# Transposes of gathered rows placed by routing groups instead of at fixed steps, in a fused recurrence and mixture-of-experts kernel

## The chip, the cores and the metric

The kernel runs on one core of one Trainium2 chip. The metric is the device time in microseconds of one execution, as the median of several runs. A core has five engines with queues of their own: TensorE (PE, with its weight loads as PEld), VectorE (DVE), ScalarE (ACT), GpSimd (POOL) and SyncE (SP); transfers are issued from these queues to 16 DMA engines.

## What is computed

A gated recurrence over four sequences of 5056 tokens gives a row of 256 numbers for each of 20224 tokens. A router then assigns every token to one of eight experts, each taking exactly 2528 tokens, the highest logits first. Each expert is a two-layer network with 1024 hidden units.

```python
sig = 1.0 / (1.0 + np.exp(-f_logit))
f = lower_bound + (1.0 - lower_bound) * sig
for t in range(S):
    h = f[:, t] * h + (1 - f[:, t]) * x[:, t]
    y[:, t] = h
...
logits = x @ w_gate                     # x: the rows y, N = 20224
for idx in np.argsort(-logits.flatten()):
    tok, e = idx // E, idx % E
    if assigned[tok] >= 0 or counts[e] >= N // E:
        continue
    assigned[tok] = e
    counts[e] += 1
...
for e in range(E):
    mask = assigned == e
    out[mask] = np.maximum(x[mask] @ w1[e], 0.0) @ w2[e]
```

## The kernel before

**Stages.** The recurrence runs until about 165 us and leaves its rows in `hbuf` in device memory. The expert stage follows and fills the rest. Products are computed with operands split in a high and a low part (`xh`, `xl`; `w1h`, `w1l`; `hh`, `hl`; the two halves of `w2s`), so each layer takes several matmuls.

**Chunks and steps.** The tokens of an expert `k` are worked in chunks `(k, c)` of up to 512 (four tiles of 128): six chunks for experts 0 and 7, five for the others, 42 in all. A chunk has eight steps `j`, one for each block of 128 hidden units. The main loop (line 1455) counts the 336 steps as `i`. Step `i` issues `first(k, c, j)`, six matmuls into a bank `pw` of three, whose result ScalarE and VectorE move out as `hh` and `hl`; then the second layer of a step that lies up to three back (`LAG`, line 1428), `second(...)`, which adds into four banks `py`, one for each tile. So a chunk's last addition falls in step 2 of the chunk after it; there ScalarE and VectorE empty the `py` banks (`y`), and in step 3 the next chunk's second layer writes them again. `second` also puts the stores of the finished rows in the list `issues`.

**Rows for a chunk.** `gather` (line 1118) puts one transfer per tile in `issues`. It is called up to two chunks ahead. `issue` (line 1035) pops entries from that list, mostly one at the end of a step, tied to the latest evacuation of `pw`. The rows land in `xg`, of which there are three. `trans(k, c, h)` (line 1164) turns half `h` of a chunk's rows: four transposes on TensorE into one more `pw` bank, written out by ScalarE as `xh` and by VectorE as `xl`. For `h == 0` it first issues what gathers of the chunk are still in the list. A chunk of two tiles is turned whole in one call, and the call for `h == 1` returns. The loop calls `trans` for the next chunk in fixed steps: 3 and 5 (`TJ`), or 5 and 6 (`T0`) in the first and last chunk of experts 0 and 1 (lines 1478 to 1481). Between a chunk's first turn and its next chunk's start lie a few steps.

**Routing beside the experts.** The assignment for the later experts is computed while the earlier ones run. Generators (`route`, `compact`, the weight split `split`) are wrapped in `Bg`; each `yield` names the engine that its next piece starts with and the tiles that it needs. `tick` (line 1435), called at several places inside `first` and `second` and at the end of a step, lets a generator go on when a model of the engines' time, `Pace`, says that the inputs are there. Pieces that name PE issue the routing groups: 20 or 23 short matmuls `rt<-O,MK` of a threshold search, the single ones `rt<-CR,tot` and `rt<-Z,onesr`, the counts `rt<-cnt,...`, and one to three placement matmuls `rt<-RA,g`. A new `Bg` starts with the need `("PE",)`, though its first piece may issue no matmul.

**Evacuations.** `post` and `flush` hold the evacuations back until `Pace` finds their input ready, or until two steps later. The order on every engine is the order in which the program issues: there is no other reordering.

All instructions are recorded from one helper, so every row of the profile carries line 109; they are told apart by their tiles.

Of the kernel before, what the change touches and what calls it, by code (L numbers as in the profile page):

```python
# [115 lines left out]
def kernel(ctx: ExitStack, tc: tile.TileContext, x: bass.AP, f_logit: bass.AP,  # L116
# [878 lines left out]
    with tc.manual_schedule(engines={mybir.EngineType.PE, mybir.EngineType.DVE, mybir.EngineType.Activation}):  # L995
        moe(ctx, tc, locals())


def moe(ctx, tc, g):
# [30 lines left out]
    issues = []  # L1030

    gate = []
    SYNC = mybir.DependencyInfo(mybir.DependencyClass.Sync, mybir.DependencyReason.DATA)

    def issue(n=1, upto=None, paced=False):
        st = None
        if upto is not None:
            n = max([x + 1 for x, (what, _) in enumerate(issues) if upto(what)], default=0)
        for _ in range(min(n, len(issues))):
            st = issues.pop(0)[1]()  # L1040
            if paced and gate:

                tc.add_manual_dep(st.ins, gate[-1].ins.name, SYNC, reason="one transfer per step")
        return st
# [25 lines left out]
    def split(k):  # L1070
        if k:
            issue(upto=lambda what: what == ("w", k))
# [37 lines left out]
    def tiles(k, c):  # L1110
        b, n = CHUNKS[k][c]
        return [min(P, CAP - (b + q) * P) for q in range(n)]
# [26 lines left out]
    posts, step = [], 0  # L1139

    def post(eng, tiles, emit, up=None, now=False):

        p = Post(eng, tiles, emit, up)
        posts.append(p)
        if now:
            flush(step)
        return p.done if now else p

    def flush(upto=-9):
        for p in list(posts):  # L1150
            if p.at <= upto or p.ready():
                p.done = p.emit() or True
                posts.remove(p)

    def turn2(t):
        return t.rearrange("p m (a b) -> p m a b", a=2)

    def pairs(t):
        return t.rearrange("p m (b a) -> p m a b", a=2)
# [4 lines left out]
    def trans(k, c, h, now=False):  # L1164
        ns = tiles(k, c)
        w, m = sum(ns), 2 if len(ns) <= 2 else 1
        if h == 0:
            issue(upto=lambda what: what == ("g", k, c))
            XS[k, c] = (xp.tile([P, 2, 512], F32R, name="xh"), xp.tile([P, 2, 512], F32R, name="xl"))
        elif m == 2:  # L1170
            return
        xh, xl = (turn2(t)[:, h:h + m, :, :w // 2] for t in XS[k, c])
        if now:
            def part(q):
                pt = pws.tile([P, 512], F32R, name="pw")
                pt = pt[:, :2 * P].rearrange("p (m w) -> p m w", m=2)
                for i in range(2):
                    nc.tensor.transpose(pt[:, i], XG[k, c][:, q, i * P:(i + 1) * P], ident_r)
                pt = pairs(pt.bitcast(F32))
                qh, ql = (t[:, :, :, q * P // 2:(q + 1) * P // 2] for t in (xh, xl))  # L1180
                up = post("ACT", (pt,), lambda: nc.scalar.activation(qh, pt, AF.Copy), None, now)
                post("DVE", (xh,), lambda: v.tensor_tensor(ql, pt, qh.bitcast(F32), op=OP.subtract), up, now)
            return [part(q) for q in range(2)]
        pt = pws.tile([P, 512], F32R, name="pw").rearrange("p (m w) -> p m w", m=m)
        for q, n in enumerate(ns):
            for i in range(m):
                nc.tensor.transpose(pt[:, i, q * P:q * P + n], XG[k, c][:n, q, (h + i) * P:(h + i + 1) * P],
                                    ident_r[:n, :n])
        pt = pairs(pt.bitcast(F32)[:, :, :w])
        up = post("ACT", (pt,), lambda: nc.scalar.activation(xh, pt, AF.Copy), None, now)  # L1190
        return post("DVE", (xh,), lambda: v.tensor_tensor(xl, pt, xh.bitcast(F32), op=OP.subtract), up, now)

    def first(k, c, j):
        w = sum(tiles(k, c))
        w1h, w1l, _ = WS[k]
        xh, xl = XS[k, c]
        ps = pws.tile([P, 512], F32, name="pw")
        mm = [(w1h, xh, 0), (w1h, xl, 0), (w1l, xh, 0), (w1h, xh, 1), (w1h, xl, 1), (w1l, xh, 1)]
        if (k, c) == (0, 0):
            mm = [(w, x, h) for w, x in ((w1h, xh), (w1l, xh), (w1h, xl)) for h in range(2)]  # L1200
        for i, (a, b, h) in enumerate(mm):
            nc.tensor.matmul(ps[:, :w], a[:, h, j], woven(turn2(b)[:, h, :, :w // 2]), start=(i == 0), stop=(i == 5))
            if i in (1, 3):
                tick()
        hh = hp.tile([P, 512], F32R, name="hh")
        hl = hp.tile([P, 512], F32R, name="hl")
        def evacuate():
            gate.append(nc.scalar.activation(hh[:, :w], ps[:, :w], AF.Relu))
        up = post("ACT", (ps,), evacuate)
        post("DVE", (hh,), lambda: v.scalar_tensor_tensor(hl[:, :w], ps[:, :w], 0.0, hh[:, :w].bitcast(F32),  # L1210
                                                          op0=OP.max, op1=OP.subtract), up)
        HS[k, c, j] = hh, hl
# [45 lines left out]
    def second(k, c, j):  # L1258
# [19 lines left out]
        for q, n in enumerate(ns):  # L1278
# [3 lines left out]
            if q:  # L1282
                tick()
# [20 lines left out]
            if q % 2 == 0:  # L1304
                turn = len(SC) // 2 + sum(what[0] == "s" for what, _ in issues) // 2
                issue(upto=lambda what: what[0] == "s" and what[1] <= turn - BEHIND)
                Y[q // 2] = yp.tile([P, 2, D], F32, name="y")
# [14 lines left out]
    class Bg:  # L1322
# [3 lines left out]
        def tick(self, force=False, within=None):  # L1326
            if self.done:
                return False
            if within is not None:
                self.wait = min(self.wait, int(within))  # L1330
            wants = bank in self.need
            if not force:
                if self.wait:
                    self.wait -= 1
                    return False
                if wants and bank.holder not in (None, self):
                    return False
                tiles = [t for t in self.need[1:] if t is not bank]
                if not pace.due(self.need[0], [*tiles, *bank.last] if wants else tiles, TIGHT if closing else SLACK):
                    return False  # L1340
            if wants:
                while bank.holder not in (None, self):
                    bank.holder.tick(True)
                bank.holder = self
            try:
                self.need = next(self.gen)
                self.wait = self.apart
            except StopIteration:
                self.done = True
            return True  # L1350

        def until(self, ok):
            while not ok():
                self.tick(True)

    comp, prog = {}, {}

# [19 lines left out]
    def have(k, what, n=1):  # L1377
        return k in prog and prog[k].get(what, 0) >= n
# [45 lines left out]
    order = [(k, c) for k in range(E) for c in range(len(CHUNKS[k]))]  # L1424
# [5 lines left out]
    TJ, T0 = (3, 5), (5, 6)  # L1430
# [24 lines left out]
    for i in range(len(todo) + LAG):  # L1455
        step = i
        flush(i - 2 if i < len(todo) else i)
        if i < len(todo):
            k, c, j = todo[i]
            if (c, j) == (0, 0) and k:  # L1460
                assert wn == k + 1
                sp.until(lambda: sp.done)
                sp = None
            first(k, c, j)
            if not sp0.done:
                flush()
            sp0.tick(True)
            tick()
            NS = len(CHUNKS[k])
            if gathers:  # L1470

                kk, cc = gathers[0]
                ahead = order.index((kk, cc)) - order.index((k, c))
                if ahead == 1 and j >= 1 or ahead == 2 and j >= (2 if (k, c) == (0, 0) else 0) and have(
                        kk, "ids", sum(CHUNKS[kk][cc])):
                    gather(kk, cc, (1, 4) if (kk, cc) == (0, 2) else None, soon=ahead == 1 or c == len(CHUNKS[k]) - 2 and j > 0)
                    gathers.pop(0)
            at = T0 if k < 2 and c in (0, NS - 1) else TJ
            nxt = order.index((k, c)) + 1
            if j in at and nxt < len(order):  # L1480
                trans(*order[nxt], at.index(j))
        while made < first_lag.get(i, i - LAG + 1):
            second(*todo[made])
            made += 1
        issue(1 if i < len(todo) else 99, paced=i < len(todo))
        tick()
# [30 lines left out]
```

## Time and profile before

| | us |
|---|---|
| median of 3 runs | 1104.24 |
| lowest and highest | 1103.49, 1104.25 |
| the profiled execution | 1103.94 |
| its span, first to last instruction | 1102.2 |
| TensorE busy in the span | 1083.9 (98%) |
| VectorE busy | 802.7 (73%) |
| ScalarE busy | 534.3 (48%) |
| GpSimd busy | 445.5 (40%) |

The profile is of one execution. Busy time is the union of an engine's instructions; a matmul's row is longer than the time for which it holds the queue, because matmuls overlap. So for TensorE the difference between one start and the next is read, not the length of a row. In a timeline, like instructions in a row are merged in one row with their count, and the row's start is that of the first.

### The profile page before, as it was taken

The numbers are of one execution on the slowest core, as the hardware profiler recorded it, in microseconds if no ns is written. First come the engines' busy times: TensorE is split into PE (matmuls) and PEld (weight loads), VectorE is DVE, ScalarE is ACT, GpSimd is POOL, SyncE is SP. The second block draws the span as 40 slices with busy tenths as digits, with TensorE's granted clock in tenths as the row PEclk, the third lists the DMA queues.
The fourth block names the chain that finished last, engine by engine and source line by source line (L and its number), as shares of the span: only waits on it lengthen the run. The fifth ranks groups of instructions, "written<-read, shape, count | busy, mean of one in ns | idle before, by whom it ended". The sixth has DMA issues, their size and how long they took to land.

```text
span 1102.2 us, 21571 instructions
## 1 busy us (share of the span) xinstructions
PE 1083.9 (98%) x8193; PEld 958.5 (87%) x8193; DVE 802.7 (73%) x2048; ACT 534.3 (48%) x1223; POOL 445.5 (40%) x428
## 2 busy tenths in 40 slices
PE   8999998999999999999999999999999999999998
PEld 6888787999988898888888888888888888898897
DVE  7999878878877896789678877887787664334333
ACT  7999775332732454245424642364226573323322
POOL 6777405332533333344333333433343433333332
PEclk9999998999999999999999999999999999999999
DMA  9999794112111311131113111311112211111110
GB/s 373 410 398 385 270 383 159 54 38 99 60 48 44 114 49 48 39 119 58 44 43 114 48 48 44 117 51 48 43 61 106 98 71 52 47 48 52 44 52 38
DMA packets 36524, 121.74 MB, mean 110 GB/s; under 512 B 7746, under 2 KB 7748, under 8 KB 35524
## 3 DMA queue, kind: packets, MB, share of 16 engines
q0 software_dynamic: 18992, 58.22, 15.3%
q1 hardware_dynamic: 17424, 62.14, 14.4%
q8 instruction: 64, 1.05, 0.4%
q14 instruction: 40, 0.33, 0.1%
q10 hardware_dynamic: 4, 0.00, 0.0%
HBM read 78.92 MB, written 41.42 MB: 109 GB/s over the span
## 4 chain that ended last, share of the span: by engine, by line
PE 91%; DMA 3%; issue 2%; DVE 1%; ACT 1%; POOL 1%; POOLq 0%; ACTq 0%; DVEq 0%
PE py L109 39%; PE pw L109 39%; PE rt L109 4%; PE pb L109 2%; PE pf L109 2%; PE pl L109 2%; PE pr L109 2%; DMA fl<-in_f_logit_dram 1%; DMA xg<-hbuf,gid 1%; DMA r<-in_moe_w_dram,wi 1%; DVE gk L109 0%; DVE fl L109 0%; ACT fl L109 0%; POOL xg L109 0%; DVE MK L109 0%
## 5 line engine op out<-in xcount | busy, mean ns | idle before, releaser
L109 PE MATMUL py<-w2s,hh 128*128 128x512 f32 (+3 forms) x1448 | 453.3, 365 | 0.0
L109 ACT ACTIVATE hh<-pw 128x512 fp32r<-128x512 f32 (+3 forms) x336 | 192.3, 572 | 439.9 <-PE pw L109 400.3
L109 PE MATMUL py<-w2s,hl 128*128 128x256 f32 (+1 forms) x1280 | 349.3, 273 | 0.0
L109 DVE SCALAR_TENSOR_TENSOR hl<-pw,hh 128x512 fp32r<-128x512 f32 (+3 forms) x336 | 219.0, 654 | 127.3 <-ACT hh L109 126.2
L109 PEld LDWEIGHTS py<-w2s,hh 128*128 128x128 f32 (+1 forms) x1448 | 261.3, 188 | 26.3
L109 POOL DMA_INDIRECT out_dram<-y,ids x160 | 161.1, 1007 | 271.9 <-ACT hh L109 143.2
L109 POOL DMA_INDIRECT xg<-hbuf,gid x160 | 161.5, 1009 | 270.9 <-ACT hh L109 211.1
L109 PE MATMUL pw<-xh,w1l 128*128 128x512 f32 (+3 forms) x672 | 249.3, 373 | 0.0
L109 PE MATMUL pw<-xl,w1h 128*128 128x512 f32 (+3 forms) x672 | 249.0, 373 | 0.0
L109 PE MATMUL pw<-xh,w1h 128*128 128x512 f32 (+3 forms) x672 | 248.3, 372 | 0.5 <-ACT xh L109 0.5
L109 PEld LDWEIGHTS py<-w2s,hl 128*128 128x128 f32 (+1 forms) x1280 | 243.1, 190 | 4.3
L109 PEld LDWEIGHTS pw<-xh,w1h 128*128 128x128 f32 x672 | 127.8, 191 | 16.0 <-ACT xh L109 0.7
L109 PEld LDWEIGHTS pw<-xh,w1l 128*128 128x128 f32 x672 | 127.8, 191 | 13.3
L109 PEld LDWEIGHTS pw<-xl,w1h 128*128 128x128 f32 x672 | 128.5, 192 | 6.9
L109 POOL TENSOR_TENSOR xl<-fl,xl 128x1024 f32<-128x1024 f32 (+2 forms) x39 | 91.2, 2347 | 27.5 <-DVE A L109 5.3
L109 DVE TENSOR_TENSOR_SCAN gk<-fg,gk,pb 128x512 f32<-128x512 f32 (+3 forms) x68 | 81.6, 1239 | 9.3 <-PE pb L109 6.9
L109 ACT ACTIVATE y<-py 128x256 f32<-128x256 f32 (+2 forms) x151 | 52.7, 409 | 71.6 <-PE py L109 65.4
L109 DVE TENSOR_TENSOR y<-py,y 128x256 f32<-128x256 f32 (+1 forms) x139 | 52.7, 418 | 41.3 <-ACT y L109 41.0
L109 ACT ACTIVATE junk<-rt,r 128x158 bf16<-128x158 f32 x155 | 59.2, 396 | 15.4 <-DVE R L109 11.4
L109 ACT ACTIVATE fg<-pf,nomlb 128x512 f32<-128x512 f32 (+1 forms) x80 | 53.9, 690 | 9.1 <-DVE gk L109 4.0
L109 DVE TENSOR_TENSOR xl<-pw,xh 128x512 fp32r<-128x512 f32 (+3 forms) x81 | 54.1, 667 | 0.2 <-ACT xh L109 0.2
L109 ACT ACTIVATE xh<-pw 128x512 fp32r<-128x512 f32 (+3 forms) x81 | 47.6, 587 | 3.8 <-PE pw L109 3.8
(224 smaller groups left out, 1255.4 us busy)
## 6 DMA issues: line engine op xcount, KB each, us to landing
fl<-in_f_logit_dram SPq DMA_DIRECT2D x39, 512.0 KB, 7.4
xl<-in_x_dram SPq DMA_DIRECT2D x39, 512.0 KB, 6.6
hbuf<-hr SPq DMA_DIRECT2D x39, 512.0 KB, 4.5
xg<-hbuf,gid POOLq DMA_INDIRECT x160, 2.7
out_dram<-y,ids POOLq DMA_INDIRECT x160, 2.4
r<-in_moe_w_dram,wi POOLq DMA_INDIRECT x25, 5.0
fl<-in_f_logit_dram SPq DMA_DIRECT2D x1, 256.0 KB, 8.0
xl<-in_x_dram SPq DMA_DIRECT2D x1, 256.0 KB, 6.2
```

The lines of the kernel that those rows point to most:

```text
L109: r = self.pace.last[self.name] = f(*args, **kw)
```

## The change

The steps 3 and 5 become windows. When step 0 of a chunk has run, two entries are put in a list `turns`, one for each half of the next chunk, with a first and a last step: 2 to 4 and 4 to 6, or exactly 5 and exactly 6 where `early` holds. Each time a `Bg` has issued a piece whose need named PE, `join` looks at the head of the list: if its first step has come and the chunk has `landed`, which means that its last gather was issued at least two steps ago and none is left in `issues`, the half is turned at once, directly behind that piece. The other half cannot follow before the next step. A half that finds no such piece is turned in its last step, behind `first` as before, and a `tick` follows it. `issue` notes for every chunk the step of its latest gather.

```diff
+    issued = {}
+
     def issue(n=1, upto=None, paced=False):
...
-            st = issues.pop(0)[1]()
+            what, emit = issues.pop(0)
+            st = emit()
+            if what[0] == "g":
+                issued[what[1:]] = step
...
+            small = self.need[0] == "PE"
             try:
                 self.need = next(self.gen)
                 self.wait = self.apart
             except StopIteration:
                 self.done = True
+            if small:
+                join()
             return True
...
+    turns = []
+
+    def landed(kc):
+        return issued.get(kc, step) <= step - 2 and not any(what == ("g", *kc) for what, _ in issues)
+
+    def join():
+        if turns and turns[0][0] <= step and landed(tuple(turns[0][2:4])):
+            turn_next()
+
+    def turn_next():
+        trans(*turns[0][2:])
+        turns.pop(0)
+        if turns:
+            turns[0][0] = max(turns[0][0], step + 1)
...
-            at = T0 if k < 2 and c in (0, NS - 1) else TJ
             nxt = order.index((k, c)) + 1
-            if j in at and nxt < len(order):
-                trans(*order[nxt], at.index(j))
+            if j == 0 and nxt < len(order):
+                early = k < 2 and c in (0, NS - 1)
+                for h, (a, b) in enumerate(((5, 5), (6, 6)) if early else ((2, 4), (4, 6))):
+                    turns.append([i + a, i + b, *order[nxt], h])
+            if turns and turns[0][1] <= i:
+                turn_next()
+                tick()
```

## Rows read from the trace of the kernel before

**Rows 1.** The page: TensorE's busy time, its granted clock in slices, the chain by engine.

```profile
PE 1083.9 (98%) x8193; PEld 958.5 (87%) x8193; DVE 802.7 (73%) x2048; ACT 534.3 (48%) x1223; POOL 445.5 (40%) x428
...
PEclk9999998999999999999999999999999999999999
...
PE 91%; DMA 3%; issue 2%; DVE 1%; ACT 1%; POOL 1%; POOLq 0%; ACTq 0%; DVEq 0%
```

**Rows 2.** Waits of TensorE's weight loads, 196 to 1098 us: total us, times, longest.

```profile
PEld rt L109 <- DVE CR L109: 0.4, 1, 0.4
```

**Rows 3.** Timeline of TensorE (start, length in us, instruction): a routing group alone.

```profile
565.18 0.38 PE L109 MATMUL pw<-xl,w1h 128*128 128x512 f32 x1
565.40 0.76 PE L109 MATMUL rt<-O,MK 128*128 128x64 bf16 x20
566.00 0.46 PE L109 MATMUL pw<-xh,w1l 128*128 128x512 f32 x1
566.30 0.38 PE L109 MATMUL pw<-xh,w1h 128*128 128x512 f32 x1
```

**Rows 4.** Timeline of TensorE: four transposes alone, between the two layers.

```profile
563.29 0.46 PE L109 MATMUL pw<-identr,xg 128*128 128x128 f32 x4
563.59 0.45 PE L109 MATMUL py<-w2s,hh 128*128 128x512 f32 x1
563.87 0.27 PE L109 MATMUL py<-w2s,hl 128*128 128x256 f32 x1
```

**Rows 5.** Timeline of TensorE: transposes that stood directly behind a routing group, two places.

```profile
453.26 0.76 PE L109 MATMUL rt<-O,MK 128*128 128x64 bf16 x20
453.85 0.51 PE L109 MATMUL pw<-identr,xg 128*128 128x128 f32 x4
454.20 0.45 PE L109 MATMUL py<-w2s,hh 128*128 128x512 f32 x1
454.49 0.27 PE L109 MATMUL py<-w2s,hl 128*128 128x256 f32 x1
...
847.46 0.38 PE L109 MATMUL rt<-RA,g 128*128 128x160 bf16 x3
847.63 0.51 PE L109 MATMUL pw<-identr,xg 128*128 128x128 f32 x4
847.98 0.47 PE L109 MATMUL py<-w2s,hh 128*128 128x512 f32 x1
848.28 0.27 PE L109 MATMUL py<-w2s,hl 128*128 128x256 f32 x1
```

**Rows 6.** Timeline of TensorE: a placement group of three, alone.

```profile
388.28 0.38 PE L109 MATMUL rt<-RA,g 128*128 128x160 bf16 x3
388.45 0.46 PE L109 MATMUL py<-w2s,hh 128*128 128x512 f32 x1
388.75 0.27 PE L109 MATMUL py<-w2s,hl 128*128 128x256 f32 x1
```

**Rows 7.** Timeline of TensorE: routing groups in the windows of (3,1) and of (6,1).

```profile
535.86 0.24 PE L109 MATMUL rt<-RA,g 128*128 128x160 bf16 x1
...
541.80 0.17 PE L109 MATMUL rt<-CR,tot 128*128 128x8 f32 x1
...
894.95 0.38 PE L109 MATMUL rt<-RA,g 128*128 128x160 bf16 x3
```

**Rows 8.** Timeline of GpSimd: the last gather of chunk (5,4).

```profile
837.34 0.92 POOL L109 DMA_INDIRECT xg<-hbuf,gid  x1 [1.72 <-ACT hh L109]
```

**Rows 9.** Timelines of VectorE and TensorE: a pass for `xl`, the next chunk's first matmul.

```profile
1044.84 0.68 DVE L109 TENSOR_TENSOR xl<-pw,xh 128x512 fp32r<-128x512 f32 x1
...
1050.29 0.38 PE L109 MATMUL pw<-xh,w1h 128*128 128x512 f32 x1
```

**Rows 10.** Timelines of VectorE and TensorE: `py` emptied and written, chunks (1,1), (7,2).

```profile
330.68 1.40 DVE L109 TENSOR_TENSOR y<-py,y 128x256 f32<-128x256 f32 x4
330.95 0.46 PE L109 MATMUL pw<-identr,xg 128*128 128x128 f32 x4
332.29 0.38 PE L109 MATMUL py<-w2s,hh 128*128 128x512 f32 x1
...
1036.93 1.09 DVE L109 TENSOR_TENSOR y<-py,y 128x256 f32<-128x256 f32 x3 [0.34 <-ACT y L109]
...
1039.17 0.38 PE L109 MATMUL py<-w2s,hh 128*128 128x512 f32 x1
```

## The prediction

> **What bounds the kernel now.** I read the page first, then the waits of TensorE's weight loads, then the timeline of TensorE alone. The page shows TensorE busy for 98% of the span, the full granted clock from end to end of the expert stage, and a chain of work that is 91% TensorE [rows 1]. So an edit pays only if it shortens TensorE's own queue, and costs only if it makes that queue wait. From 196 to 1098 us, where the expert stage runs steadily, almost no wait is left: the longest of a weight load, behind VectorE's `CR`, is 0.4 us, once [rows 2]. What remains to be won is time that TensorE loses between two kinds of work with no wait in the records.
>
> That loss is seen by comparing starts. A 512-column matmul frees the queue after 0.22 us (565.18 to 565.40). The first one behind a routing group of 20 short matmuls holds it for 0.30 (566.00 to 566.30): an exit of 0.08, once per group. Group and exit, with that matmul, take 0.90 [rows 3]. Four transposes on their own hold 0.30 and the matmul behind them 0.28 (563.29, 563.59, 563.87), together 0.58 [rows 4].
>
> **What the change removes, adds and moves.** No instruction is added or removed on any engine. The two calls of `trans` for the next chunk leave steps 3 and 5 and go behind the first routing group found in steps 2 to 4 and 4 to 6; without one they go out behind the first layer of step 4 or 6, with one more `tick()` after them. Chunks with `early` keep steps 5 and 6.
>
> *The price of one join.* The trace of before holds joins by accident, where a group ended just ahead of the old place; I found six in the steady part and show two. With 20 `O,MK` matmuls, group, transposes and the first long matmul take 453.26 to 454.49, 1.23 us. Apart they are 0.90 + 0.58, in which one long matmul, 0.22, is counted twice: 1.26. Saved: 0.03 [rows 3 to 5]. With a placement group `rt<-RA,g`: apart 0.47 + 0.58 - 0.22 = 0.83, joined 847.46 to 848.28, 0.82 [rows 4 to 6]. Rounded rows leave 0.01 to 0.02 either way. The mechanism is visible: the exit of 0.08 falls away, and in exchange the transposes last 0.35 instead of 0.30 [rows 4, 5]. I take 0.03 for `O,MK` and 0.02 for `RA,g`. For the groups of single matmuls, `CR,tot` and `cnt`, I show no row; they lie between no gain and the whole exit of 0.08, and since they too end in very short matmuls I take the 0.03 of `O,MK`.
>
> *How many joins.* For each of the 41 chunks that are transposed inside the loop I listed which routing groups start in its two windows. Chunk (3,1), transposed during (3,0), shows how: `RA,g` stands at 535.86 in step 2, `CR,tot` at 541.80 in step 4, so its halves join these two. The last window with a group is that of (6,1), with the one at 894.95 [rows 7]. Counted so, 47 of the 79 sets of transposes have a group: 19 `RA,g`, 17 `O,MK`, 6 `CR,tot`, 5 `cnt`. The condition on gathers excludes few, since most chunks have their last gather before the window opens. The tightest is (5,4): the gather starts at 837.34, in step 1, so step 2 is refused and only the second half joins [rows 8].
>
> The sum: 19 x 0.02 + 28 x 0.03 = 1.22 us. Six are joined already (five worth 0.03, one 0.02), 0.17. That leaves **1.05 us** from 41 new joins. The weight split and compaction of an expert begin with a piece that counts as TensorE's in the code but issues no matmul; some three windows may be spent on those, under 0.1 us.
>
> *What else is moved.* `trans` may issue gathers that are still listed, but a join asks that none of its chunk be left, and at the deadline one step more has passed; so POOL's queue is passed by nothing new and SP's not at all. The 32 sets without a group move one step later between the same two kinds of matmul and cost the same 0.58. What hides the delay is the lead of their evacuation: of the transposes of step 5, VectorE's pass starts at 1044.84 and lasts 0.68, and the next chunk begins at 1050.29 [rows 9]; a step later, 4.8 us of lead become about 2. If that cover were gone, TensorE would wait at the chunk's head. The extra `tick()` may set a routing group behind transposes, an order of which I show no row: each is worth between a loss and a gain of the transposes' own exit, 0.28 - 0.22 = 0.06. Windows without a group have few pieces ready, and I take zero.
>
> *A cover that the move takes away.* Step 2 ends the second layer of the chunk before. Its four `py` banks are emptied by ScalarE and VectorE while step 3 runs its first layer and, until now, the transposes. In step 3 of (1,1) the transposes start at 330.95; VectorE's four passes over `py` end at 330.68 + 1.40 = 332.08, and TensorE writes the fourth bank at 332.29: a lead of 0.21. Without the transposes' 0.30 there it is a stall of 0.09. In the part without routing the same lead is 1.15 (1036.93 + 1.09 to 1039.17) [rows 10]. I book one stall of 0.1 for the short lead: 1.05 - 0.10 = 0.95.
>
> The Trainium skill, in "TensorE: Matmul & The Clock Gate", section "LDWEIGHTS (loading the stationary operand)", puts a weight load at its columns over 1.2 GHz, which is 107 ns for 128. By that, an estimate, four transposes without the cover of a long matmul would last 0.43 us and a join would lose 0.05. The joined row shows 0.35 [rows 5], so the measurement decides against it as a forecast.
>
> **The rivals.** *Slower through `py`.* The place is the first writes of `py` in step 3 after a join in step 2; twelve windows of experts 1 to 6 have a group in that step. The price: the lead, less 0.30, less an evacuation of 0.68 that now falls ahead of the emptying. At a lead of 0.21 that is a stall of 0.77, at 1.15 none; in the middle 0.38, for twelve 4.6, giving 1104.24 - 1.05 + 4.6 = 1107.8. Three such stalls cancel the gain; nine make the kernel 0.2% slower. For it: the lead of 0.21. Against it: leads near 1.15, and that transposes of step 2 can be evacuated before the first `py` is done.
>
> *Slower through uncovered loads.* One exposed load can be read as 0.03 for the last short matmul (0.60 for 20) plus the exit of 0.08 [rows 3]. Were all four loads of every new join exposed so, they would last 0.44 instead of 0.35, and a join would lose 0.06: in sum 2.5, 1106.7. The page's rule above comes to the same; the joined row speaks against both.
>
> *Half the joins.* The code releases routing by modelled times, and every join shifts what follows; groups can slip out of their windows. Half of 1.05 gives 1103.7. It is also the case in which the change hardly does what it says.
>
> *More than the sum.* The wait of 0.4 behind `CR` [rows 2] need not come back, and with two-digit rows a join may be worth 0.02 more, 0.8 in all: 1102.1 with both, 1102.7 with half.
>
> **How the numbers follow.** The profiled execution took 1103.94 us with a span of 1102.2, and the median of the three runs is 1104.24, 0.3 above it. The span should go to 1101.2, the profiled time to 1103.0, the median to 1104.24 - 0.95, so **1103.3**. Chances: forecast 0.59 (1102.5 to 1104.1), half the joins 0.14, more than the sum 0.12, slower through `py` 0.13, uncovered loads 0.02. The range of 1102.0 to 1105.0 takes in the first two, most of the third and of the fourth the cases with up to four stalls; about 0.15 is left out. A measurement of this kernel tells about 0.2%, 2.2 us, from no change. Faster than that needs the end of the third case or the edge of the forecast: 0.08. Slower needs nine stalls or uncovered loads: 0.08. Within 0.2%: 0.84.
>
> **What would show it.** In the trace after, most transposes up to 900 us should have an `rt` row directly ahead and last about 0.35, and the group ahead of them should have lost its exit; those after 905 should stand in steps 4 and 6 at 0.30. No wait on `y`, `xl` or a gather should appear at TensorE's weight loads. The forecast is wrong if fewer than 30 groups are joined, if the writes of `py` in step 3 come late, if the first layer of a chunk waits for `xl`, or if the granted clock falls.

## The result, and the profile after

The changed kernel takes 1114.55 us (median of six runs, 1111.22 to 1118.0) against 1103.93 for the kernel before in runs on the same chip: a ratio of 1.0097, 95% interval 1.0075 to 1.0119. It is slower by some 10 us where a gain of 1 was forecast. Its profiled execution took 1111.22 us, span 1109.5, 7.3 more than the profiled one of before; it was the shortest of the six.

The page of the changed kernel: busy times, granted clock, the chain by engine and by line, and the additions of the second layer (busy us, mean ns | idle before them, what ended most of it).

```profile
PE 1084.4 (98%) x8193; PEld 958.3 (86%) x8193; DVE 801.5 (72%) x2048; ACT 537.1 (48%) x1223; POOL 446.6 (40%) x428
...
PEclk9999999999999999999999999999999999999999
...
PE 80%; DMA 5%; issue 5%; DVE 3%; POOL 3%; ACT 2%; SPq 0%; POOLq 0%; ACTq 0%; DVEq 0%
PE py L109 34%; PE pw L109 34%; PE rt L109 4%; PE pb L109 2%; DMA r<-in_moe_w_dram,wi 2%; PE pl L109 2%; PE pf L109 2%; DMA xg<-hbuf,gid 1%; PE pr L109 1%; POOL xg L109 1%; POOL r L109 1%; DMA hbuf<-hr 1%; DMA xl<-in_x_dram 1%; DVE hl L109 1%; ACT y L109 1%
...
L109 PE MATMUL py<-w2s,hh 128*128 128x512 f32 (+3 forms) x1448 | 450.6, 364 | 4.8 <-DVE y L109 4.5
```

Counts and clock are as before, and TensorE is busy 0.5 us more [rows 1]. The chain fell from 91% TensorE to 80%, and what it lost went to transfers, to evacuations and, with 1% each, to GpSimd's issuing of gathers (`xg`) and of the load of raw expert weights (`r`). The waits of TensorE's weight loads, 196 to 1109 us of the span (total us, times, longest), name two places:

```profile
PEld py L109 <- DVE y L109: 7.4, 8, 1.4
...
PEld pw L109 <- DMA xg<-hbuf,gid: 2.0, 3, 1.0
PEld py L109 <- ACT y L109: 0.7, 1, 0.7
```

Before, the longest wait was 0.4 [rows 2]. From the differences of matmul starts I read what each place costs the queue, beyond what the matmul ahead takes:

| place | us | what stood in front |
|---|---|---|
| `py` in step 3 of (1,1), (4,1), (5,1) | 0.80, 1.03, 1.04 | a routing pass `MK`, then `xl`, ahead of `hl` and `y` on VectorE |
| `py` in step 3 of (2,3) | 0.89 | weight split `w1h` ahead of `xh`, `hh` and `y` on ScalarE; with them came `xl`, ahead of `hl` and `y` on VectorE |
| `py` in step 3 of (1,3) | 0.22 + 1.31 | the 1.31: weight split `w1h` ahead of the fourth `y` on ScalarE |
| `py` in step 3 of (3,3), (4,3) | 0.45, 0.38 | weight split: at (3,3) `w1h` ahead of `hh` and `y` on ScalarE, at (4,3) `w1l` ahead of `y` on VectorE |
| transposes in (0,5), (3,0), (5,0) | 0.45, 1.04, 0.67 | a gather that had not landed |

Together 8.3. From the start of chunk (0,2) to the last addition the changed kernel takes 7.46 us longer: its waits over 0.1 us grew from 0.72 to 9.23, and the rest of TensorE's queue became **1.05 shorter**. After 905 us the two kernels run alike: the chunk that began at 943.09 begins at 950.48, the one at 1050.29 [rows 9] at 1057.67, 7.4 later each time.

Four places, by the timelines of the changed kernel (start, length in us, instruction, wait in brackets). First (1,1), VectorE and then TensorE:

```profile
329.44 0.78 DVE L109 TENSOR_TENSOR MK<-K,TH 128x1200 bf16<-128x1200 int16 x1
330.14 0.69 DVE L109 TENSOR_TENSOR xl<-pw,xh 128x512 fp32r<-128x512 f32 x1
330.74 0.68 DVE L109 SCALAR_TENSOR_TENSOR hl<-pw,hh 128x512 fp32r<-128x512 f32 x1
331.34 1.41 DVE L109 TENSOR_TENSOR y<-py,y 128x256 f32<-128x256 f32 x4
...
330.79 0.38 PE L109 MATMUL pw<-xh,w1l 128*128 128x512 f32 x1
331.81 0.48 PE L109 MATMUL py<-w2s,hh 128*128 128x512 f32 x1 [0.64 <-DVE y L109]
```

In the kernel before VectorE went from `MK` over `hl` to `y`, whose passes began at 330.68, 1.30 behind the start of `MK`, and TensorE turned rows at 330.95 meanwhile [rows 10]:

```profile
329.38 0.78 DVE L109 TENSOR_TENSOR MK<-K,TH 128x1200 bf16<-128x1200 int16 x1
330.08 0.68 DVE L109 SCALAR_TENSOR_TENSOR hl<-pw,hh 128x512 fp32r<-128x512 f32 x1
```

Now the `xl` of the half joined in step 2 holds VectorE from 330.14 to 330.74, `y` begins at 331.34, 1.90 behind the start of `MK`, and TensorE, with no transposes left in step 3, stands from 331.01 to 331.81.

Second (4,1), VectorE and TensorE before and then after. Step 3 begins at 677.65 before and at 682.20 after:

```profile
676.24 0.78 DVE L109 TENSOR_TENSOR MK<-R,thr 128x1200 bf16<-128x1200 int16 x1
678.38 1.08 DVE L109 TENSOR_TENSOR y<-py,y 128x256 f32<-128x256 f32 x3
...
680.29 0.38 PE L109 MATMUL py<-w2s,hh 128*128 128x512 f32 x1
```

```profile
682.16 0.78 DVE L109 TENSOR_TENSOR MK<-R,thr 128x1200 bf16<-128x1200 int16 x1
682.86 0.68 DVE L109 TENSOR_TENSOR xl<-pw,xh 128x512 fp32r<-128x512 f32 x1
683.46 0.68 DVE L109 SCALAR_TENSOR_TENSOR hl<-pw,hh 128x512 fp32r<-128x512 f32 x1
684.06 1.41 DVE L109 TENSOR_TENSOR y<-py,y 128x256 f32<-128x256 f32 x4
...
684.53 0.48 PE L109 MATMUL py<-w2s,hh 128*128 128x512 f32 x1 [0.87 <-DVE y L109]
```

Before, the last of the passes over `py` ended 1.81 after the step's start (679.46), and the fourth bank was written 0.83 later. After, they end 3.27 after the step's start. Of the 1.46 between, 0.60 is the `xl` pass. The rest goes with routing's `MK`, which began 1.41 ahead of the step and now begins 0.04 ahead of it. So the lead of 0.83 was used up by two things, the evacuation and a background pass that had moved. (5,1) looks the same.

Third (1,3), ScalarE and TensorE. `w1h` waited for its raw weights, and `y`, behind it on ScalarE, waited too:

```profile
380.01 1.23 ACT L109 ACTIVATE w1h<-r,omlb 128x512 fp32r<-128x512 f32 x1 [1.73 <-DMA r<-in_moe_w_dram,wi]
381.14 0.36 ACT L109 ACTIVATE y<-py 128x256 f32<-128x256 f32 x1
...
382.01 0.48 PE L109 MATMUL py<-w2s,hh 128*128 128x512 f32 x1 [1.14 <-DVE y L109]
```

Fourth (3,0), GpSimd's gathers for (3,1), and TensorE:

```profile
534.11 0.98 POOL L109 DMA_INDIRECT xg<-hbuf,gid  x1 [1.65 <-ACT hh L109]
...
542.41 0.94 POOL L109 DMA_INDIRECT xg<-hbuf,gid  x1 [1.92 <-ACT hh L109]
...
536.63 0.38 PE L109 MATMUL rt<-RA,g 128*128 128x160 bf16 x3
...
543.95 0.37 PE L109 MATMUL pw<-identr,xg 128*128 128x128 f32 x3
545.17 0.28 PE L109 MATMUL pw<-identr,xg 128*128 128x128 f32 x1 [0.85 <-DMA xg<-hbuf,gid]
545.30 0.24 PE L109 MATMUL rt<-RA,g 128*128 128x160 bf16 x1
```

The chunk began at 531.74 (before at 528.83). In the kernel before its placement ended with the `RA,g` at 535.86 [rows 7], 7.0 after the chunk's start; now the same group stands at 545.30, 13.6 after it. Routing itself has slipped. The gathers for (3,1), which had all gone out in the chunk before ((3,0) minus 5.7 for the last, 523.15), now go out in steps 0 to 3 of (3,0), the last 10.7 after its start; it lands as the transposes at their deadline stand at the head of TensorE's queue. The code has a path for this: chunks two ahead are gathered only if `have` finds their `ids` assigned, else a chunk later. That the slip of routing leads through this path is read from code and order, not tried by itself.

### The profile page after: what moved, and what is told of

Read it like the earlier page. It is cut to its first block, busy times and chain, and to the rows that moved or that the text cites. A ratio compares the mean times of both kernels' runs of the same rounds, so it can differ in the third digit from the quotient of the medians.

```text
span 1109.5 us, 21572 instructions
## 1 busy us (share of the span) xinstructions
PE 1084.4 (98%) x8193; PEld 958.3 (86%) x8193; DVE 801.5 (72%) x2048; ACT 537.1 (48%) x1223; POOL 446.6 (40%) x428
## 3 DMA queue, kind: packets, MB, share of 16 engines
q8 instruction: 64, 1.05, 0.4%
## 4 chain that ended last, share of the span: by engine, by line
PE 80%; DMA 5%; issue 5%; DVE 3%; POOL 3%; ACT 2%; SPq 0%; POOLq 0%; ACTq 0%; DVEq 0%
PE py L109 34%; PE pw L109 34%; PE rt L109 4%; PE pb L109 2%; DMA r<-in_moe_w_dram,wi 2%; PE pl L109 2%; PE pf L109 2%; DMA xg<-hbuf,gid 1%; PE pr L109 1%; POOL xg L109 1%; POOL r L109 1%; DMA hbuf<-hr 1%; DMA xl<-in_x_dram 1%; DVE hl L109 1%; ACT y L109 1%
```

## The experiments

The theories: **(A)** `py`: whatever comes ahead of `y` on ScalarE and VectorE around step 2, with the transposes gone from step 3, makes the next chunk's first addition wait. **(B)** Gathers: transposes reach TensorE before their rows have landed. **(C)** The extra `tick()`, taken at zero, shifts the split of weights and with it `y`. **(D)** The joins themselves cost. No kernel here leaves any work out. Kernels sent together share a chip and the runs of the kernel before; in the second set that kernel took 1106.5 us, in the others 1103.7 to 1104.1, so ratios are compared.

**The measure.** In each trace I take TensorE's time from the start of chunk (0,2) to the last addition and split it in waits over 0.1 us (a start that comes later than the columns ahead explain) and the rest. Stretches in which the granted clock is at its lower level count as waits too; late36 and t4 have one each. "Joined" counts sets of transposes with an `rt` group directly ahead, of 79; ratios stand with their 95% interval.

| kernel | joined | waits | rest | ratio |
|---|---|---|---|---|
| before | 9 | 0.72 | 883.57 | 1 |
| after | 46 | 9.23 | 882.52 | 1.0097 (1.0075 to 1.0119) |
| again | 46 | 12.69 | 882.68 | 1.010 (1.007 to 1.013) |
| late | 11 | 4.79 | 883.35 | 1.0022 (1.0012 to 1.0032) |
| from3 | 42 | 3.86 | 882.96 | 1.0006 (0.9997 to 1.0016) |
| hold | 49 | 3.29 | 882.99 | 1.0015 (1.0005 to 1.0025) |
| stay3 | 31 | 9.20 | 882.92 | 1.0042 (1.0029 to 1.0056) |
| late36 | 7 | 6.55 | 883.53 | 1.0010 (1.0001 to 1.0019) |
| t2 | 4 | 12.82 | 884.05 | 1.0104 (1.0089 to 1.0120) |
| t4 | 6 | 21.98 | 884.18 | 1.0146 (1.0131 to 1.0162) |
| gwait | 47 | 9.30 | 882.71 | 1.0060 (1.0039 to 1.0080) |
| hold3 | 42 | 3.10 | 882.80 | 1.0011 (1.0002 to 1.0021) |
| hold0 | 41 | 16.01 | 882.56 | 1.0125 (1.0108 to 1.0142) |
| hold023n | 38 | 9.96 | 882.62 | 1.0103 (1.0086 to 1.0120) |
| notick | 39 | 12.51 | 883.00 | 1.0114 (1.0099 to 1.0130) |
| s35n | 16 | 0.82 | 883.54 | 1.0002 (0.9993 to 1.0011) |
| s34n | 23 | 2.91 | 883.42 | 1.0023 (1.0014 to 1.0033) |

**The changed kernel again**, unaltered.

> The changed kernel unaltered, for a second profile of it. Theory A (TensorE waits for the py banks in step 3, since the transposes have left that step and their VectorE pass xl, joined in step 2, stands ahead of the emptying): again some 6 us of waits ahead of py matmuls, at the same chunks, and a time of 1111 to 1118. Theory B (routing comes later, so gathers are issued later and transposes wait for their landing): some 2 us of waits inside the transposes, which vary from run to run with the transfers. If the runs' spread comes from transfers, the py waits of this profile equal those of the first one within 0.5 us and the rest differs.

Ratio 1.010. The second profile (span 1113.3) waits at the same places, 7.7 us at `py` and 3.5 at gathers, 2.4 of these at (5,0) where the first had 0.67. So the loss is the program's. Of its 3.5 us more of waits 1.6 are at `py` and 1.3 at gathers, so the waits at `py`, expected to agree within 0.5, did not.

**No joins, but the later steps.**

```diff
     def join():
-        if turns and turns[0][0] <= step and landed(tuple(turns[0][2:4])):
-            turn_next()
+        return
```

> No joins: every half is turned in the last step of its window, 4 and 6, with the tick behind it. 11 sets stand behind a routing group by accident, against 46. Theory A: the transposes have left step 3, which takes 0.30 us from each lead, but no xl stands ahead of the emptying in step 2, so only the shortest leads turn into waits: below 1 us of py waits, 1104 to 1105. Theory B: the later steps give gathers more time, no waits inside transposes: 1104. Theory C (it is the fixed later steps and the additional tick that cost, not the joins): 1110 or more.

Ratio 1.0022, waits at `py` of 3.1 us ((1,3) 1.27 + 0.50, (2,1) 0.87), none at gathers. Steps 4 and 6 with the extra `tick()` alone cost some 2.4 us without any join: there is a part of the loss that no join makes. No theory had it. At (1,3) no evacuation of a joined half stands ahead of `y`, but the weight split does, `w1h` twice and `w1l`; at (2,1) a routing pass `MK` does.

**First windows from step 3.**

```diff
-... ((2, 4), (4, 6))
+... ((3, 4), (4, 6))
```

> The first window begins at step 3 instead of step 2, all else as changed; 42 sets still stand behind a routing group. Theory A: without step 2 the xl pass no longer stands ahead of the emptying; the py waits fall from 6.1 us to below 2, and the time to 1104 to 1106. Theory B: gathers still come late where routing does, 2 us of waits inside transposes: 1106. Theory C (each join costs, where it was priced as a gain): 42 joins of 46 remain, so 9/10 of the loss: about 1113.

Ratio 1.0006, no measurable difference. With 42 joins, none in step 2, waits at `py` fall to 1.1 and those at gathers vanish. So neither the number of joins nor the deadline in steps 4 and 6 is what costs 10 us; against (D), and for step 2.

**`xl` held behind the second layer of the chunk before.** Joins as in the changed kernel, step 2 too; only the pass that writes `xl` may not be issued before that layer's last addition.

```diff
-            return (self.up is None or self.up.done) and pace.due(...)
+            return made >= self.behind and (self.up is None or self.up.done) and pace.due(...)
...
-        return post("DVE", (xh,), ..., up, now)
+        return post("DVE", (xh,), ..., up, now, step // FB * FB)
```

> Joins as changed, step 2 included, but the VectorE pass xl of transposes is held back until the second layer of the chunk before has been issued whole, so it stands behind the emptying of py. Theory A: of each py wait up to 0.68 us goes; at the five waits of 0.8 to 1.0 us some 0.3 stays, from the 0.30 that left step 3: py waits of 1.5 to 3 us, 1107 to 1110. If the place of xl on VectorE has no part in it, py waits stay at 6 us. Theory B alone: unchanged, 1114.

Ratio 1.0015 with 49 joins, 15 of them in step 2. The waits at (1,1) and (4,1) are gone, the one at (5,1) fell from 1.04 to 0.43, and no gather is late. The time is below the 1107 to 1110 of theory A, so more went than the `xl` pass. That looks like a cure, but see hold0 below.

**The old steps moved without joins or ticks.** The kernel before, with only its fixed steps changed.

```diff
-    TJ, T0 = (3, 5), (5, 6)
+    TJ, T0 = (2, 5), (5, 6)
```

> The kernel before with one number changed: the first half is turned in step 2 instead of 3, with no join and no further tick. Theory A: both parts of the loss without any join: py waits of 5 us or more where routing runs beside, none after 905 us, where the lead of 1.15 holds 0.30 and 0.68; 1109 to 1114. If it is the joins that cost: 1104.

Ratio 1.0104: the same loss with 4 joins instead of 46. TensorE waits 1.07 at the first `py` of step 3 in (2,1), (3,1), (4,1) and (5,1), four equal places in the part where experts repeat. The timelines of VectorE and TensorE at (2,1):

```profile
449.42 0.78 DVE L109 TENSOR_TENSOR MK<-R,thr 128x1200 bf16<-128x1200 int16 x1
450.12 0.68 DVE L109 SCALAR_TENSOR_TENSOR hl<-pw,hh 128x512 fp32r<-128x512 f32 x1
450.72 0.68 DVE L109 TENSOR_TENSOR xl<-pw,xh 128x512 fp32r<-128x512 f32 x1
451.32 1.41 DVE L109 TENSOR_TENSOR y<-py,y 128x256 f32<-128x256 f32 x4
...
451.88 0.45 PE L109 MATMUL py<-w2s,hh 128*128 128x512 f32 x1 [0.90 <-DVE y L109]
```

The transposes of step 2 send their own evacuation (`xl` here, 0.60 between starts) ahead of `y`, behind a routing pass `MK` that stands there too. It needs no join. The four places make 4.3 of this kernel's 12.8 us of waits, gathers 1.7; the rest is scattered.

```diff
-    TJ, T0 = (3, 5), (5, 6)
+    TJ, T0 = (4, 5), (5, 6)
```

> The kernel before with the first half turned in step 4 instead of 3, no join, no further tick. Theory A: only the first part, 0.30 us less lead: py waits of 2 to 3 us at the chunks whose lead was short, 1106 to 1107, and less than with step 2. If the additional tick was the cause in the run with steps 4 and 6: 1104.

Ratio 1.0146, the worst of all, and a miss for every theory that puts the loss in step 2 alone. Its waits have several causes, and the largest is not in this list (weight loads of this kernel, 196 to 1109 us):

```profile
PEld pw L109 <- DVE hl L109: 5.2, 7, 1.2
PEld rt L109 <- DVE Z L109: 4.8, 3, 1.6
...
PEld pw L109 <- DMA xg<-hbuf,gid: 3.7, 3, 1.6
PEld py L109 <- ACT hh L109: 3.1, 3, 1.0
```

The largest is the clock of this execution. TensorE stood 1.2 and 1.7 us for gathers at (0,5), and from 298.1 to 308.3 the granted clock is then 0.50, its level of 1.2 GHz. The same matmuls, from the first addition behind those transposes to the fourth matmul of (1,0), take 9.40 us here and 4.60 in the changed kernel: some 4.8 of the 21.98. The profiled execution is the longest of four, 1126.6 against 1121.9 to 1124.6, so the other three may have lost less in this way.

The waits for a `pw` bank (5.2) fit transposes in two steps running, which take two of the three banks while the first layer needs them. But at (1,2), where one of them is, four routing passes `MK` stand ahead of the needed `hl` on VectorE, so the transposes alone are not shown to make it. At `py` the three places are (3,1), (4,1) and (5,1), 0.83 each: at (3,1) `MK` and `hl` stand ahead of `y` on VectorE, and no evacuation of transposes does. A routing pass that has moved can thus make such a wait alone.

**First half only in step 3, second half 4 to 6; and steps 3 and 6 with no joins.**

```diff
-... ((2, 4), (4, 6))
+... ((3, 3), (4, 6))
```

> The first half is turned in step 3 only, joined if a routing group ends the first layer there and behind it otherwise, so always ahead of the first py writes; the second half joins in steps 4 to 6. 31 sets stand behind a group, against 9 before. Theory A (the loss is the cover of py in step 3, in two parts: the transposes' own 0.30 us and the xl pass ahead of the emptying): no py wait is added, 22 new joins at 0.025 give 0.55 less than before, 1103.5. Theory C (joins cost): above before, 1106 or more. If routing's pace is what counts (theory B), waits inside transposes and 1105.

Ratio 1.0042, a miss, and `py` waits 3.2 us where none had been expected, 2.0 of them at (3,3) with `w1l` and `w1h` ahead of `y`. With the second half joined already in step 4, transposes wait for a `pw` bank (3.6 us behind `hl`). The longest, at (2,3) of this kernel, is shown for TensorE; the `hl` of the needed bank stands behind `w1l` and routing passes on VectorE:

```profile
500.48 0.52 PE L109 MATMUL pw<-identr,xg 128*128 128x128 f32 x4 [1.77 <-DVE hl L109]
```

> No joins; the first half in step 3 as before, the second in step 6 instead of 5, each with the additional tick behind it. It differs from the run with steps 4 and 6 by the first half alone. Theory A: the transposes are back in step 3, so the py waits of that run (3.1 us) go: 1104.0 to 1104.5. If the tick or the later second half cost: 1106 to 1107, as there.

(`join` returns at once, windows (3, 3) and (6, 6).) Ratio 1.0010, at the limit of what can be told. No wait at `py` is left in step 3, but a routing group of (0,4) waits 3.0 behind ScalarE, and behind that wait the granted clock is 0.50 from 280.6 to 284.0, which costs some 1.5 us more. This execution is the longest of ten (1110.4, the shortest 1106.3). The kernel is not told apart from the one without joins at steps 4 and 6.

**Deadline moved up to two steps while gathers are not landed.**

```diff
-            if turns and turns[0][1] <= i:
+            if turns and turns[0][1] <= i and (landed(tuple(turns[0][2:4])) or turns[0][1] + 2 <= i):
```

> As changed, but a half whose gathers were not issued two steps ago waits up to two steps longer for its deadline. Only chunks with late gathers differ. Theory B (late gathers are their own part of the loss, beside py): the waits inside transposes in experts 3 and 5 (1.0 and 0.7 to 2.4 us in the two profiles of the changed kernel) go, py waits stay at 6 to 8: 2 to 3 us less than as changed, a ratio of 1.007. If the transposes' wait only covered another wait behind it, the ratio stays at 1.0095.

Ratio 1.006. No wait on a gather is left, against 2.2 and 3.5 in the two profiles of the changed kernel, and the median is some 4 us lower, though the two intervals overlap a little. That theory B holds for this share is likely and not shown by the profile: its span is 1109.5 like that of the changed kernel's first profile, because other waits grew by what the gathers no longer cost. 7.3 us at `py` stay, 2.7 of them at (1,3) behind `w1h`.

**Holding `xl`, in other surroundings.** Hold with windows (3, 4) and (4, 6); hold with expert 0 kept at steps 3 and 5; and that again with windows (2, 3), (4, 5) and no extra `tick()`.

> Both remedies in one: windows from step 3 and the pass xl behind the second layer of the chunk before. In windows that begin in step 3 the second layer of the chunk before has been issued already, so holding back should change nothing there: ratio as with step 3 alone, 1.0006, within 0.001. If holding back works through something other than the place of xl against y in step 2, it adds its own difference.

Ratio 1.0011, waits at `py` of 1.0: no better than either edit alone.

> xl held back, and expert 0 with its fixed steps 3 and 5 again. 41 sets stand behind a group. The profile with xl held back had 1.1 us of wait ahead of a placement group in (0,4), where only expert 0's new order differs: without it 1.0 us less, ratio 1.0005. If that wait is chance of the run, the ratio stays at 1.0015.

Ratio 1.0125, a miss: the schedule of expert 0 alone turns the 1.5 us of hold into 14. `py` waits 7.4 us (2.59 at (1,3)), transposes 7.0 for gathers. So the small loss of hold was in part a lucky order. But three places can be compared with the changed kernel one to one, since in both the half is joined in step 2 behind the same kind of group: (1,1), (4,1) and (5,1) waited 0.80, 1.03 and 1.04, and wait 0.21, 0.43 and 0.44 here, 0.6 less each. VectorE at (1,1) of this kernel, then TensorE:

```profile
332.14 0.78 DVE L109 TENSOR_TENSOR MK<-K,TH 128x1200 bf16<-128x1200 int16 x1
332.84 0.68 DVE L109 SCALAR_TENSOR_TENSOR hl<-pw,hh 128x512 fp32r<-128x512 f32 x1
333.44 0.75 DVE L109 TENSOR_TENSOR y<-py,y 128x256 f32<-128x256 f32 x2
...
333.49 0.38 PE L109 MATMUL pw<-xh,w1l 128*128 128x512 f32 x1
333.91 0.48 PE L109 MATMUL py<-w2s,hh 128*128 128x512 f32 x1
```

From `MK` to `y` are 1.30 us here and 1.90 in the changed kernel; the 0.60 between is the `xl` pass. The 0.21 that remain are of the kind that the prediction booked: the cover of transposes that left step 3. The 0.43 and 0.44 at (4,1) and (5,1), where the lead before was 0.83, are more than that cover of 0.30; there the moved `MK` is left. And (2,3) still waits 0.65 with its `xl` held, so the most of its 0.89 is not `xl`.

> Joins that keep the covers: first half in step 2 or 3 (never later), second in 4 or 5, xl held back behind the emptying, expert 0 as before, no additional tick. 38 sets behind a group against 9: 29 x 0.026 = 0.75 us less than before if no wait is added, ratio 0.9993. By theory A nothing is left that lengthens a py wait but the 0.30 us of the joins in step 2; with those ratio up to 1.001. If shifts of the issue order alone bring waits wherever they fall, 1.002 or more.

Ratio 1.0103, a miss as well. No gather is late, yet `py` waits 7.8 us: 3.0 at (1,3), and 0.43 at (2,1), (3,1), (4,1) and (5,1).

**The extra `tick()` taken out.**

```diff
                 turn_next()
-                tick()
```

> The changed kernel with the one tick behind transposes at their last step taken out; windows and joins are as changed. It tells what the extra tick() cost, which the prediction took at zero. If the weight split and the compaction stand ahead of y because of the extra tick, the waits at py behind w1l or w1h ((1,3), (3,3), (4,3), (5,3): some 4 us in the changed kernel) go, and the waits behind xl at (1,1), (4,1), (5,1) (2.9 us) stay: ratio 1.005 to 1.007. If the tick is worth nothing, as predicted, the ratio stays at 1.009 to 1.011 and the same places wait. If it is the only cause, the ratio is 1.000 or below.

Ratio 1.0114, not told apart from the changed kernel. The waits at the places of the weight split stay ((1,3) 0.23 + 1.54, (3,3) 0.20 + 0.50, (4,3) 0.38, (5,3) 0.50). Theory C falls: the `tick()` is not what puts the split ahead of `y`.

**The steps kept, with and without room.** Windows of one step, 3 and 5, and no extra `tick()`: the old places, with a join where a group stands in that step anyway. Then 3 and 4 to 5.

> The smallest shift that still joins: windows of one step each, 3 and 5, as in the kernel before, without the extra tick; transposes go behind a routing group of that same step if there is one, else to their old place. About 16 of 84 sets are joined instead of 9, so the joins are worth some 0.2 us. If the loss of the change comes from moving the transposes to other steps (py left without its cover in step 3, routing and gathers later), this kernel keeps its waits at py and at gathers within 1 us and the ratio is 0.998 to 1.001. If any new order at all re-deals who stands ahead of y, waits of 3 us or more come up at places of their own: ratio 1.003 or above.

> Windows 3 (one step) and 4 to 5, without the extra tick: some 23 sets joined, none in step 2, none later than before. Some 0.4 us from joins. By the theory that the steps moved to make the loss (step 2 for py, steps 4 and 6 for gathers), ratio 0.998 to 1.001, waits within 1.5 us; transposes in steps 3 and 4 one behind the other need a bank pw sooner, and if that decides, weight loads behind hl wait 3 us or more, ratio 1.003 or above.

With the old steps (s35n) the ratio is 1.0002, and the profile has no wait at `py` or at gathers; of weight loads, 196 to 1109 us, these are the longest:

```profile
PEld L109 <- issue: 14.0, 58, 0.4
PEld L109 <- DVE hl L109: 3.1, 13, 0.2
PEld rt L109 <- DVE CR L109: 0.4, 1, 0.4
```

That is the list of the kernel before, with its one 0.4 behind `CR` [rows 2]. The seven more joins at the old places re-deal nothing, and with the 42 joins of from3, which cost nothing measurable, (D) is out. One step of freedom for the second half (s34n), with 7 more joins, brings 0.6 and 0.2 back at `py` and a wait of 1.1 of transposes in step 4 for their bank, and 1.0023, more than the moved steps alone were expected to cost.

No variant beats the kernel before: s35n and from3 equal it, the others are slower.

## Why the prediction was wrong, step by step

*The price and the number of joins were right.* 46 sets are joined (47 were counted from the trace of before). Nine stood so before, not six, so 37 joins are new and not 41. The rest of TensorE's time fell by 1.05 us in the first profile and 0.89 in the second, for a sum of 1.05. Over the 17 traces of the table a straight line gives 0.027 us less rest for each set joined (standard error 0.003, scatter of one trace 0.23). It is a fit over kernels that differ in other things too (0.022 without t2 and t4); the 7 additional joins of s35n, worth 0.2 by it, show 0.03, which that scatter allows. A joined set, on TensorE of the changed kernel, is as it was [rows 5]:

```profile
452.86 0.76 PE L109 MATMUL rt<-O,MK 128*128 128x64 bf16 x20
453.45 0.52 PE L109 MATMUL pw<-identr,xg 128*128 128x128 f32 x4
453.80 0.45 PE L109 MATMUL py<-w2s,hh 128*128 128x512 f32 x1
```

The transposes hold 0.35. The rival of uncovered loads is out, and with it the estimate of 0.43 worked out from the section "LDWEIGHTS (loading the stationary operand)" of "TensorE: Matmul & The Clock Gate" in the Trainium skill: the trace differs.

*"A cover that the move takes away" is the step that failed.* It booked one stall of 0.1 for `py`, from the transposes' 0.30 alone. In the profile `py` waits 6.1 us at seven chunks, for three reasons:

- The evacuation follows the transposes into step 2 and, the engines running in issue order, stands ahead of `y` unless something holds it back: 0.60 each at (1,1), (4,1) and (5,1) by hold0, and 0.24 of the wait at (2,3), about 2.0 together.
- Pieces of the weight split now stand ahead of `y`: 1.31 at (1,3), 0.83 at (3,3) and (4,3), and most of the other 0.65 at (2,3), about 2.8.
- The remaining 1.3, at (1,1), (1,3), (4,1) and (5,1), is the lost cover that was booked, together with routing passes that now stand ahead of `y`. The two are not told apart.

So step 2 was priced as if only the transposes left step 3. The rival through `py` did price the evacuation, at a lead of 0.21 as 0.77, and (1,1), the chunk with that lead, shows 0.80: the price was known. It was given 0.13 because the lead elsewhere is 1.15. That row is from the part without routing, and no join in step 2 happens there. But the leads of the routed part would not have named the places either. In the trace of before the fourth bank's lead is 0.83 at (4,1) and (5,1), for which the rival's formula gives 0.15, and they wait 1.03 and 1.04. It is 0.56 at (2,2) and (6,0), for which the formula gives 0.42, and they wait for nothing. A lead of before is not the lead after, since the background pieces ahead of `y` move as well.

*The rival's sum came close by luck.* It booked 4.6 us in twelve windows. Twelve chunks had their first half turned in step 2; five of them, (1,1), (1,3), (2,3), (4,1) and (5,1), wait 5.3 us at `py` in step 3, and seven wait for nothing. Of the 5.3, 2.2 are at (1,3) and (2,3), most of it behind the split and not behind an evacuation of transposes. With 0.83 more at (3,3) and (4,3) this is a mechanism the prediction did not have: moving the transposes changes when `Pace` lets every background piece go, and the weight split, 1.2 us a piece, may then land ahead of `y`. The run without the extra `tick()` shows that the `tick()` is not its cause, and late, with `w1h` and `w1l` ahead of `y` at (1,3), that moved steps suffice without joins. Why a given piece falls where it does was not settled.

*"POOL's queue is passed by nothing new" was the other false step.* No gather was moved past another, but the routing that gathers depend on came later, and the gathers with it: 2.2 and 3.5 us of waits in the two profiles, and a median some 4 us lower in the run that waits for landing, as far as overlapping intervals tell. A landed condition guards the joins; the deadline turns rows whether they have landed or not.

*The extra `tick()` at zero* held, as far as 0.2% can tell. *One step later at no cost* held where no routing runs: after 905 us the transposes stand in steps 4 and 6 and every chunk keeps its distance. In the routed part it did not hold: late loses 2.4 us with no joins to speak of. The prediction booked them at nothing because TensorE's own queue does not change by them; the order on the other engines does.

*What was to show it.* "Wrong if the writes of `py` in step 3 come late" is what happened; the clock did not fall, and `xl` kept no first layer waiting.

Account of the profiled execution: waits of 9.23 us, of which 6.1 at `py`, 2.2 at gathers and 0.9 in small ones, less the 0.72 of before and less 1.05 for the joins, make 7.46; the span grew by 7.3. The median lies 3.3 above that execution; the second profile, with 3.5 us more of waits, is nearer to it.

## What to carry to other kernels

When instructions move in a kernel whose engines run in issue order, price what they bring along on the other engines (here the evacuation and the background work that fills the gap) against the shortest lead of the buffers there, read in the stage that is touched and not in a quieter one. Even then the lead in the old trace is only a first guess: background work moves with the edit, and at (4,1) a lead of 0.83 was gone. All 37 new joins, at 0.03 us each, pay for little more than one wait of 0.8. Test a merge first at the place where both parts already stand, as s35n does: it tells the price of merging from the price of moving.

## What the runs showed of the hardware

One thing was not expected: the same gather, issued at the same distance from its chunk's start (10.8 us) in two executions of one program, let the transposes go 3.15 us after its issue in one and 4.91 in the other; it had landed 3.11 and 4.86 us after it. GpSimd's issue and TensorE's transposes of (5,0), first in the changed kernel, then in its second profile:

```profile
776.65 0.95 POOL L109 DMA_INDIRECT xg<-hbuf,gid  x1 [1.78 <-ACT hh L109]
...
779.80 0.28 PE L109 MATMUL pw<-identr,xg 128*128 128x128 f32 x1 [0.47 <-DMA xg<-hbuf,gid]
```

```profile
777.43 0.95 POOL L109 DMA_INDIRECT xg<-hbuf,gid  x1 [1.78 <-ACT hh L109]
...
782.34 0.28 PE L109 MATMUL pw<-identr,xg 128*128 128x128 f32 x1 [2.22 <-DMA xg<-hbuf,gid]
```

In both TensorE would have been ready about 2.5 us after the issue, and stood 0.67 and 2.39. In the kernel before gathers landed 2.5 to 4.7 us after their start, 2.7 in the median, so a lead of 2.5 us is not enough, and one of 3 not always. The changed kernel's times spread from 1111 to 1118 us, where the kernel before keeps within 1102.8 to 1104.5. That the gathers make this spread is not shown: gwait, which has no wait on a gather, spreads from 1108.1 to 1112.7, and t2, with 1.7 us of such waits, only from 1118.1 to 1118.8.

The other is the clock. From 196 us to 1096 the granted clock of the kernel before is 0.99 or more in every stretch of 4 us, and so it is in all but two of the runs. In these two it fell to 0.50, the level of 1.2 GHz, behind a stand of TensorE: of 3.0 us in late36, for 3.4 us, and of 1.2 and 1.7 us in t4, for 10.2 us, where the same matmuls took 9.40 us instead of 4.60. The stand of 2.39 above was followed by no fall. So a wait can cost more than its own length, and need not.
